# Softmax scaling of a dynamic convolution moved from VectorE to GpSimd, behind the pace of its products

## The chip, the cores and the metric

One core of a Trainium2 chip. The metric is the device time of one execution in microseconds (us), lower is better. All runs told here are fast, with a granted TensorE clock of 0.987 to 1.0. Ratios are the mean time of one kernel's fast runs over that of the other's fast runs of the same rounds, so they are not quite the ratio of the medians that are quoted. Spans in profiles are about 2 us shorter than times.

Names: TensorE is PE in the profile (PEld its weight loads), VectorE is DVE, ScalarE is ACT, GpSimd is POOL, SyncE is SP.

## The reference, cut to what matters

```python
# per token and head: softmax over K = 7 taps, then a weighted sum of 7 shifted rows of x
w = np.exp(weight_gen - max);  w = w / w.sum(-1)            # (8, 4096, 8 heads, 7)
conv = einsum('bshk,bskhg->bshg', w, x_unfolded)            # D = 192 = 8 heads x 24
h = conv.reshape(32768, 192) @ w_in                         # 192 -> 2048
out = (h - tanh(h)) @ w_out                                 # 2048 -> 192
```

## The kernel before

Tokens go through in 32 superblocks of 1024. In iteration n of the main loop, TensorE makes the first matmul of superblock n (16 tiles `ph`), the second matmul of superblock n-1 (into `obank`), and, at the seventh of eight pairs of tiles, the sums of superblock n+1 (`conv`: the products are added up while they are transposed, into `pc`). ScalarE does tanh, exp and copies, VectorE does `h - tanh(h)` (`gt`) and the softmax of superblock n+3, GpSimd the seven products of superblock n+2 and an accumulating transfer that adds the odd products to the even ones. The "pace" is an ordering: GpSimd's work for superblock n+2 may not start before VectorE's second subtraction of iteration n.

```python
def softmax_norm(n, bank, in_psum=False):
    e_t, zsum = softmax_sum(n)                    # reduction on VectorE
    zr = bank[:, 512 - J * H : 512]               # a corner of the PSUM bank of the sums
    nc.vector.reciprocal(zr, zsum[:])
    ...
    wsm = wgpool.tile([P, J, H, K], FP32, name="wsm")
    last_wsm[0] = scale(nc.vector, wsm[:], e_t, zr)
    wsm_of[n] = (wsm, wsm_v)
...
# in products(n, ..., behind): 7 multiplications on GpSimd
            if k == 0 and behind is not None:
                order(mul, behind, "pace")        # not before the second subtraction of the iteration
...
for n in range(NTOT):
    if n + 3 < NTOT:
        load_wg(n + 3)
        load_x(n + 3)                             # xpool has 2 buffers: waits for products(n + 1)
    for p in range(J):
        gemm1(n, 2 * p)
        gemm1(n, 2 * p + 1)
        ...
        if p == 0 and 1 <= n < NTOT - 2:
            products(n + 2, behind=last_sub[0] if n > 1 else None)
        if n + 1 < NTOT:
            if p == (6 if n > 0 else 7):
                conv(n + 1, (0, 1))
            if p == (6 if n > 1 else 7):
                bank = conv(n + 1, (2,))
        ...
        if p == (7 if n == 1 else 6) and n + 3 < NTOT:
            softmax_norm(n + 3, bank if n > 0 else obank[0])
```

The `ph` and `pc` tiles share three PSUM buffers in rotation.

The softmax here doesn't subtract the row's maximum and nothing guards it: scores larger than these inputs give would overflow.

Of the kernel before, what the change touches and what calls it, by code (L numbers as in the profile page):

```python
# [8 lines left out]
FP32 = mybir.dt.float32  # L9
# [7 lines left out]
def kernel(  # L17
# [8 lines left out]
    nc = tc.nc  # L26

    B, S, D = x.shape
    H, K = weight_gen.shape[2], weight_gen.shape[3]
    G = D // H  # L30
    F = moe_w_in.shape[1]
    P = nc.NUM_PARTITIONS
# [3 lines left out]
    J = 8  # L36
# [4 lines left out]
    NTOT = B * NSB  # L41
# [11 lines left out]
    wgpool = ctx.enter_context(tc.tile_pool(name="wgpool", bufs=2))  # L53
# [11 lines left out]
    obank = [psum_o.tile([P, 512], FP32, name=f"obank{i}", tag=f"obank{i}") for i in range(2)]  # L65
# [6 lines left out]
    wsm_of = {}  # L72
# [8 lines left out]
    def order(inst, other, reason):  # L81
        tc.add_manual_dep(
            inst.ins,
            other.ins.name,
            mybir.DependencyInfo(mybir.DependencyClass.Sync, mybir.DependencyReason.DATA),
            reason=reason,
        )
# [44 lines left out]
    def softmax_exp(n):  # L132
        wg_t = wg_of.pop(n)
        e_t = wgpool.tile([P, J, H, K], FP32, name="e_t")
        nc.scalar.activation(  # L135
            out=e_t[:].rearrange("p j h k -> p (j h k)"),
            in_=wg_t[:].rearrange("p j h k -> p (j h k)"),
            func=ACT.Exp,
        )
        e_of[n] = e_t  # L140

    def softmax_sum(n):
        e_t = e_of.pop(n)
        zsum = wgpool.tile([P, J * H], FP32, name="zsum")
        nc.vector.reduce_sum(  # L145
            out=zsum[:], in_=e_t[:].rearrange("p j h k -> p (j h) k"), axis=AX.X
        )
        return e_t, zsum

    def softmax_norm(n, bank, in_psum=False):  # L150

        e_t, zsum = softmax_sum(n)
        zr = bank[:, 512 - J * H : 512]
        nc.vector.reciprocal(zr, zsum[:])  # L154
        wsm_v = None
        if in_psum:
            wsm_v = obank[n % 2][:, 0 : J * H * K].rearrange("p (j h k) -> p j h k", j=J, h=H)
            scale(nc.vector, wsm_v, e_t, zr)
        wsm = wgpool.tile([P, J, H, K], FP32, name="wsm")
        last_wsm[0] = scale(nc.vector, wsm[:], e_t, zr)  # L160
        wsm_of[n] = (wsm, wsm_v)

    def softmax_norm_gpsimd(n):
        e_t, zsum = softmax_sum(n)
        zr = wgpool.tile([P, J * H], FP32, name="zr")
        nc.vector.reciprocal(zr[:], zsum[:])
        wsm = wgpool.tile([P, J, H, K], FP32, name="wsm")
        scale(nc.gpsimd, wsm[:], e_t, zr[:])
        wsm_of[n] = (wsm, None)

    def scale(eng, wsm, e_t, zr):
        return eng.tensor_mul(  # L172
            wsm.rearrange("p j h k -> p (j h) k"),
            e_t[:].rearrange("p j h k -> p (j h) k"),
            zr.rearrange("p (n o) -> p n o", o=1).to_broadcast([P, J * H, K]),
        )

    def products(n, on_vector=(), sums=None, hooks={}, behind=None):
        x_t = x_of.pop(n)
        wsm, wsm_v = wsm_of.pop(n)  # L180
        in_pairs = n not in PLAIN

        even = ppool.tile([P, NPAIR, NC, J, H, GC], BF16, name="even")
        odd = ppool.tile([P, NPAIR, NC, J, H, GC], BF16, name="odd")
        last = ppool.tile([P, NC, J, H, GC], BF16, name="last")
        dst = {}
        for i in range(NPAIR):
            dst[2 * i] = even[:, i]
            dst[2 * i + 1] = odd[:, i]
        dst[K - 1] = last[:]  # L190
        if -1 in hooks:
            hooks[-1]()
        for k in range(K):
            eng, w = (nc.vector, wsm_v) if k in on_vector else (nc.gpsimd, wsm[:])
            mul = eng.tensor_mul(  # L195
                dst[k].rearrange("p c j h g -> p j h c g"),
                x_t[:, k : k + J, :].rearrange("p j (h c g) -> p j h c g", h=H, c=NC),
                w[:, :, :, k : k + 1]
                .rearrange("p j h (k o) -> p j h k o", o=1)
                .to_broadcast([P, J, H, NC, GC]),  # L200
            )
            if k == 0 and behind is not None:


                order(mul, behind, "pace")
            if k == K - 2 and in_pairs:

                nc.gpsimd.dma_start(  # L208
                    out=even[:].rearrange("p i c j h g -> p (i c j h g)")[:, 0:ACC],
                    in_=odd[:].rearrange("p i c j h g -> p (i c j h g)")[:, 0:ACC],  # L210
                    accum_op=mybir.AluOpType.add,
                    max_dma_last_dim=4096,
                )
            if k in hooks:
                hooks[k]()
        if in_pairs:
            groups = [even[:, i] for i in range(NPAIR)] + [last[:]]
            prods_of[n] = [
                groups + ([odd[:, NPAIR - 1]] if c == NC - 1 else []) for c in range(NC)
            ]  # L220
        else:
            prods_of[n] = [[dst[k] for k in (sums or range(K))]] * NC

    def conv(n, *parts):

        prods = prods_of[n]
        if n not in conv_of:
            conv_of[n] = cpool.tile([P, NC, HT], BF16, name="convT")
        convT = conv_of[n]
        pcs = [psum_h.tile([P, 2, HT], FP32, name="pc", tag="ph") for _ in parts]  # L230

        for gi in range(max(len(g) for g in prods)):
            for chunks, pc in zip(parts, pcs):
                some = [c for c in chunks if gi < len(prods[c])]
                last = gi == max(len(prods[c]) for c in chunks) - 1
                for c in some:
                    for j in range(JH):
                        col = ((c - chunks[0]) * JH + j) * R
                        for r in range(2):
                            nc.tensor.matmul(  # L240
                                pc[:, r, col : col + R],
                                lhsT=prods[c][gi][
                                    r * R : (r + 1) * R, c, 2 * j : 2 * j + 2
                                ].rearrange("p j h g -> p (j h g)"),
                                rhs=ident[r * R : (r + 1) * R, r * R : (r + 1) * R],
                                start=(gi == 0 and c == chunks[0] and j == 0),
                                stop=(last and c == some[-1] and j == JH - 1),
                            )
        for chunks, pc in zip(parts, pcs):
            c0, nch = chunks[0], len(chunks)  # L250
            nc.scalar.activation(  # L251
                out=convT[:, c0 : c0 + nch, :].rearrange("p c (j r t) -> p r (c j) t", r=2, t=R),
                in_=pc[:, :, 0 : nch * JH * R].rearrange("p r (cj t) -> p r cj t", t=R),
                func=ACT.Copy,
            )
        if parts[-1][-1] == NC - 1:
            prods_of.pop(n)
        return pcs[-1][:, 0]

    def gemm1(n, f):  # L260
        convT = conv_of[n]
# [120 lines left out]
    load_wg(0)  # L382
    load_x(0)
    softmax_exp(0)
    softmax_norm(0, obank[0], in_psum=True)
    load_wg(1)
    load_x(1)
    load_w_in(0, FA)
# [4 lines left out]
        hooks={2: rest_of_w_in},  # L393
    )
    softmax_exp(1)
    softmax_norm(1, obank[1], in_psum=True)
    load_wg(2)
    copy_w_in(0, FA, nc.scalar)
    copy_w_in(FA, F, nc.sync)
    products(1, on_vector=(0, 1), hooks={4: load_w_out})  # L400
    conv(0, (0, 1), (2,))
    load_x(2)
# [3 lines that stand above are left out]
            load_x(n + 3)  # L406
# [3 lines that stand above are left out]
            if n == 0 and p == 1:  # L410
                softmax_exp(2)
            if p == 5 and n + 3 < NTOT:
                softmax_exp(n + 3)
            if n >= 1:
                gemm2((n - 1) * J + p)
# [3 lines that stand above are left out]
                if p == (6 if n > 0 else 7):  # L419
                    conv(n + 1, (0, 1))  # L420
                if p == (6 if n > 1 else 7):
                    bank = conv(n + 1, (2,))
            if n == 0 and p == 2:
                softmax_norm_gpsimd(2)
                products(2)
            if p == (7 if n == 1 else 6) and n + 3 < NTOT:

                softmax_norm(n + 3, bank if n > 0 else obank[0])
    gemm2(LAST)
    for j in range(J):  # L430
        gemm2_last(j)
# [30 lines left out]
```

## Time and profile before

| | kernel before |
|---|---|
| time, median of 3 | 772.58 us (771.97 to 773.71) |
| span of the profile | 770.0 us |
| TensorE busy | 96%, and 93% of the chain that ended last |
| one superblock with softmax, in the steady part | 22.82 us |
| the one superblock without (end of the run) | 22.63 us |
| GpSimd idle per superblock, waiting at the pace | 1.18 us |

A superblock's time is read from TensorE: from the start of one superblock's sums to the start of the next ones. The lines are in the prediction.

### The profile page before, as it was taken

To read this page: it belongs to the slowest core of one execution; us is meant where nothing else is said; L and a number is where in the kernel's file an instruction comes from. 1 tells how busy PE (TensorE), PEld (TensorE's weight loads), DVE (VectorE), ACT (ScalarE), POOL (GpSimd) and SP (SyncE) were. 2 spreads that over 40 slices of the span, in tenths; PEclk is the share of its full clock that TensorE was granted. 3 is DMA by queue.
4 is the path that set the end of the run, shared out by engine and by line. 5 is a ranking of instruction groups with operands and counts; after the bars stand their busy time and mean duration, and the time that the engine had idled before them with its cause. 6 is when DMAs were issued, how large, how long until landed. Compare 5 with 4: busy or idle time off the path is not lost.

```text
span 770.0 us, 32309 instructions
## 1 busy us (share of the span) xinstructions
PE 740.4 (96%) x14784; PEld 578.0 (75%) x14784; DVE 668.6 (87%) x624; ACT 640.9 (83%) x865; POOL 668.3 (87%) x261
## 2 busy tenths in 40 slices
PE   2789999999999999999999999999999999999997
PEld 2267777777777777777777778777777777778777
DVE  6978989988989889888988998989889988988883
ACT  1877888888888888888888888888888888888882
POOL 6999999999999999999999999999999999999000
PEclk9999999999999999999999999999999999999999
DMA  7913677665557765556775555775555776542312
GB/s 214 196 63 96 172 182 182 164 143 127 148 147 181 182 152 125 134 149 168 181 177 114 129 155 155 181 178 134 132 142 147 177 181 156 132 118 63 81 43 84
DMA packets 25848, 111.38 MB, mean 145 GB/s; under 512 B 4800, under 2 KB 9456, under 8 KB 21624
## 3 DMA queue, kind: packets, MB, share of 16 engines
q1 hardware_dynamic: 14688, 76.95, 30.1%
q0 software_dynamic: 10816, 31.99, 25.8%
q8 instruction: 115, 1.88, 1.0%
q10 hardware_dynamic: 208, 0.39, 0.2%
q14 instruction: 21, 0.17, 0.1%
HBM read 54.49 MB, written 25.17 MB: 103 GB/s over the span
## 4 chain that ended last, share of the span: by engine, by line
PE 93%; DVE 3%; POOL 1%; DMA 1%; ACT 1%; issue 1%; SPq 0%; POOLq 0%; DVEq 0%
PE ph L265 43%; PE obank L297 43%; PE pc L240 6%; DVE gt L277 2%; PE po L331 1%; DMA x_t<-in_x_dram 1%; POOL even L195 1%; ACT convT L251 0%; ACT th L275 0%; POOL odd L195 0%; DVE wsm L172 0%; DVE zsum L145 0%; SPq L117 0%; DVE pc L154 0%; DVE obank L154 0%
## 5 line engine op out<-in xcount | busy, mean ns | idle before, releaser
L277 DVE TENSOR_TENSOR gt<-ph,th 128x1024 bf16<-128x1024 f32 x512 | 602.5, 1219 | 63.9 <-ACT th L275 63.6
L275 ACT ACTIVATE th<-ph 128x1024 f32<-128x1024 f32 x512 | 497.3, 1022 | 64.3 <-PE ph L265 63.6
L265 PE MATMUL ph<-convT,w_in 64*128 64x512 bf16 x3072 | 385.5, 377 | 7.5 <-DVE gt L277 5.3
L297 PEld LDWEIGHTS <-gt 64*128 64x128 bf16 x7936 | 344.2, 94 | 52.8 <-issue 1.1
L297 PE MATMUL obank<-w_out,gt 64*128 64x192 bf16 x7936 | 373.9, 243 | 1.8 <-issue 0.9
L195 POOL TENSOR_TENSOR even<-x_t,wsm 128x1536 bf16<-128x1536 f32 x94 | 276.8, 2945 | 29.3 <-DVE gt L277 28.2
L195 POOL TENSOR_TENSOR odd<-x_t,wsm 128x1536 bf16<-128x1536 f32 x93 | 273.8, 2945 | 0.0
L265 PEld LDWEIGHTS <-w_in 64*128 64x128 bf16 x3072 | 175.8, 94 | 117.2 <-issue 20.4
L195 POOL TENSOR_TENSOR last<-x_t,wsm 128x1536 bf16<-128x1536 f32 x31 | 103.4, 3337 | 0.0
L315 ACT ACTIVATE out_sb<-obank 128x192 f32<-128x192 f32 x248 | 82.2, 331 | 14.1 <-PE obank L297 8.7
L251 ACT ACTIVATE convT<-pc 128x1024 bf16<-128x1024 f32 x64 | 48.6, 808 | 30.8 <-PE pc L240 30.8
L240 PE MATMUL pc<-ident,even 64*128 64x64 bf16 x2304 | 47.3, 191 | 3.0 <-DVE gt L277 1.5
L240 PEld LDWEIGHTS <-even 64*128 64x128 bf16 x2304 | 42.5, 96 | 3.8 <-issue 1.9
L208 POOL DMA_DIRECT2D even<-odd x29 | 34.9, 1205 | 9.0 <-POOL odd L195 9.0
L154 DVE RECIPROCAL pc<-zsum 128x64 f32<-128x64 f32 x28 | 15.7, 561 | 14.8 <-ACT convT L251 14.8
L240 PE MATMUL pc<-ident,odd 64*128 64x64 bf16 x448 | 15.3, 198 | 12.6 <-DVE odd L195 12.4
L135 ACT ACTIVATE e_t<-wg_t 128x448 f32<-128x448 f32 x32 | 18.5, 577 | 7.6 <-DMA wg_t<-in_weight_gen_dram 7.6
L240 PE MATMUL pc<-ident,last 64*128 64x64 bf16 x768 | 23.1, 191 | 0.7 <-issue 0.6
L145 DVE TENSOR_REDUCE zsum<-e_t 128x64 f32<-128x448 f32 x32 | 19.5, 609 | 3.0 <-ACT e_t L135 3.0
L240 PEld LDWEIGHTS <-odd 64*128 64x128 bf16 x448 | 11.3, 100 | 12.9 <-DVE odd L195 12.5
L172 DVE TENSOR_TENSOR wsm<-e_t,pc 128x448 f32<-128x448 f32 x28 | 17.4, 622 | 2.9
L240 PEld LDWEIGHTS <-last 64*128 64x128 bf16 x768 | 16.9, 96 | 1.0 <-issue 0.7
(22 smaller groups left out, 51.4 us busy)
## 6 DMA issues: line engine op xcount, KB each, us to landing
x_t<-in_x_dram SPq DMA_DIRECT2D x24, 1344.0 KB
even<-odd POOLq DMA_DIRECT2D x29, 1024.0 KB, 8.9
out_dram<-out_sb SPq DMA_DIRECT2D x31, 768.0 KB
x_t<-in_x_dram SPq DMA_DIRECT2D x8, 1176.0 KB
wg_t<-in_weight_gen_dram SPq DMA_DIRECT2D x32, 224.0 KB
x_t<-in_x_dram SPq DMA_DIRECT2D x8, 157.5 KB
w_in<-in_moe_w_in_dram POOLq DMA_DIRECT2D x6, 128.0 KB, 6.7
w_out<-in_moe_w_out_dram POOLq DMA_DIRECT2D x1, 768.0 KB, 9.2
```

The source lines that it names most:

```text
L135: nc.scalar.activation(out=e_t[:].rearrange("p j h k -> p (j h k)"), in_=wg_t[:].rearrange("p j h k -> p (j h k)"), func=ACT.Exp,)
L145: nc.vector.reduce_sum(out=zsum[:], in_=e_t[:].rearrange("p j h k -> p (j h) k"), axis=AX.X)
L172: return eng.tensor_mul(wsm.rearrange("p j h k -> p (j h) k"), e_t[:].rearrange("p j h k -> p (j h) k"), zr.rearrange("p (n o) -> p n o", ...
L195: mul = eng.tensor_mul(dst[k].rearrange("p c j h g -> p j h c g"), x_t[:, k : k + J, :].rearrange("p j (h c g) -> p j h c g", h=H, c=NC), ...
L208: nc.gpsimd.dma_start(out=even[:].rearrange("p i c j h g -> p (i c j h g)")[:, 0:ACC], in_=odd[:].rearrange("p i c j h g -> p (i c j h g)" ...
L240: nc.tensor.matmul(pc[:, r, col : col + R], lhsT=prods[c][gi][r * R : (r + 1) * R, c, 2 * j : 2 * j + 2].rearrange("p j h g -> p (j h g)") ...
L251: nc.scalar.activation(out=convT[:, c0 : c0 + nch, :].rearrange("p c (j r t) -> p r (c j) t", r=2, t=R), in_=pc[:, :, 0 : nch * JH * R].re ...
L265: nc.tensor.matmul(ph[:, r, :], lhsT=w_in[r * R : (r + 1) * R, c, f * P : (f + 1) * P], rhs=convT[r * R : (r + 1) * R, c, :], start=(c == ...
L275: last_act[0] = nc.scalar.activation(out=th[:], in_=ph_f, func=ACT.Tanh)
L277: last_sub[0] = nc.vector.tensor_sub(gt[:], ph_f, th[:])
L297: mm = nc.tensor.matmul(po[:, 0:D], lhsT=g_of[n][f][r * R : (r + 1) * R, col : col + P], rhs=w_out[r * R : (r + 1) * R, f, :], start=(r == ...
L315: last_act[0] = nc.scalar.activation(out=out_sb[:, j, :], in_=po[:, 0:D], func=ACT.Copy)
```

## The change

The intent: give VectorE back the scaling (0.62 us per superblock), and put it on GpSimd in the idle time that the pace leaves it. The pace moves from the first product to the scaling ahead of it, and the reciprocal goes to SBUF, where the kernel before already keeps it for superblock 2, the one that GpSimd scales (0.97 us at 35.77 us in the prediction's fourth view).

```diff
-    def softmax_norm(n, bank, in_psum=False):
+    def softmax_norm(n, bank=None):
...
+        wsm = wgpool.tile([P, J, H, K], FP32, name="wsm")
+        if bank is None:
+            zr = wgpool.tile([P, J * H], FP32, name="zr")
+            nc.vector.reciprocal(zr[:], zsum[:])
+            wsm_of[n] = (wsm, None, e_t, zr)
+            return
...
     def products(n, on_vector=(), sums=None, hooks={}, behind=None):
         x_t = x_of.pop(n)
-        wsm, wsm_v = wsm_of.pop(n)
+        wsm, wsm_v, e_t, zr = wsm_of.pop(n)
+        if e_t is not None:
+            first = scale(nc.gpsimd, wsm[:], e_t, zr[:])
+            if behind is not None:
+                order(first, behind, "pace")
...
-            if k == 0 and behind is not None:
-                order(mul, behind, "pace")
...
-            if p == (7 if n == 1 else 6) and n + 3 < NTOT:
-                softmax_norm(n + 3, bank if n > 0 else obank[0])
+            if p == 6 and n + 3 < NTOT:
+                softmax_norm(n + 3)
```

More of the change, by code (lines that the diff above doesn't have):

```diff
@@ L140, in softmax_exp @@
         e_of[n] = e_t
-    def softmax_sum(n):
+    def softmax_norm(n, bank=None):
         e_t = e_of.pop(n)
@@ L147, in softmax_sum @@
         )
-        return e_t, zsum
-    def softmax_norm(n, bank, in_psum=False):
-        e_t, zsum = softmax_sum(n)
+        wsm = wgpool.tile([P, J, H, K], FP32, name="wsm")
[4 more added lines that the diff above has]
+            return
         zr = bank[:, 512 - J * H : 512]
         nc.vector.reciprocal(zr, zsum[:])
-        wsm_v = None
-        if in_psum:
-            wsm_v = obank[n % 2][:, 0 : J * H * K].rearrange("p (j h k) -> p j h k", j=J, h=H)
-            scale(nc.vector, wsm_v, e_t, zr)
-        wsm = wgpool.tile([P, J, H, K], FP32, name="wsm")
-        last_wsm[0] = scale(nc.vector, wsm[:], e_t, zr)
-        wsm_of[n] = (wsm, wsm_v)
-    def softmax_norm_gpsimd(n):
-        e_t, zsum = softmax_sum(n)
-        zr = wgpool.tile([P, J * H], FP32, name="zr")
-        nc.vector.reciprocal(zr[:], zsum[:])
-        wsm = wgpool.tile([P, J, H, K], FP32, name="wsm")
-        scale(nc.gpsimd, wsm[:], e_t, zr[:])
-        wsm_of[n] = (wsm, None)
+        wsm_v = bank[:, 0 : J * H * K].rearrange("p (j h k) -> p j h k", j=J, h=H)
+        scale(nc.vector, wsm_v, e_t, zr)
+        last_wsm[0] = scale(nc.vector, wsm[:], e_t, zr)
+        wsm_of[n] = (wsm, wsm_v, None, None)
     def scale(eng, wsm, e_t, zr):
@@ L194, in products @@
             eng, w = (nc.vector, wsm_v) if k in on_vector else (nc.gpsimd, wsm[:])
-            mul = eng.tensor_mul(
+            eng.tensor_mul(
                 dst[k].rearrange("p c j h g -> p j h c g"),
@@ L257, in conv @@
             prods_of.pop(n)
-        return pcs[-1][:, 0]
     def gemm1(n, f):
@@ L384 @@
     softmax_exp(0)
-    softmax_norm(0, obank[0], in_psum=True)
+    softmax_norm(0, obank[0])
     load_wg(1)
@@ L395 @@
     softmax_exp(1)
-    softmax_norm(1, obank[1], in_psum=True)
+    softmax_norm(1, obank[1])
     load_wg(2)
@@ L421 @@
                 if p == (6 if n > 1 else 7):
-                    bank = conv(n + 1, (2,))
+                    conv(n + 1, (2,))
             if n == 0 and p == 2:
-                softmax_norm_gpsimd(2)
+                softmax_norm(2)
                 products(2)
-            if p == (7 if n == 1 else 6) and n + 3 < NTOT:
-                softmax_norm(n + 3, bank if n > 0 else obank[0])
+            if p == 6 and n + 3 < NTOT:
+                softmax_norm(n + 3)
     gemm2(LAST)
```

## The prediction

> **What bounds the kernel now.** I read the page first: engine shares, then the chain that ended last.
>
> ```profile
> PE 740.4 (96%) x14784; PEld 578.0 (75%) x14784; DVE 668.6 (87%) x624; ACT 640.9 (83%) x865; POOL 668.3 (87%) x261
> PE 93%; DVE 3%; POOL 1%; DMA 1%; ACT 1%; issue 1%; SPq 0%; POOLq 0%; DVEq 0%
> ```
>
> TensorE is busy 96% of the 770.0 us span and carries 93% of the chain. VectorE and GpSimd are at 87%, so a change of theirs pays only where TensorE waits for them. GpSimd stops at 712 us (last product), so inside its stretch it is much fuller than 87%.
>
> The second view is the chain as pieces in time: one superblock with softmax work, from the transposing sums of one superblock (`pc`, x104) to the next, and then the end of the run, where no superblock is left to normalise.
>
> ```profile
> 408.82 1.52 PE pc L240 x104
> ...
> 413.15 0.65 PE ph L265 x6
> 413.80 0.02 issue
> 413.81 0.82 PE ph L265 x6
> ...
> 431.64 1.52 PE pc L240 x104
> ...
> 705.57 1.52 PE pc L240 x104
> ...
> 728.20 1.52 PE pc L240 x104
> ```
>
> Columns: start, length, what. A superblock with softmax takes 431.64 - 408.82 = 22.82 us, the one without 728.20 - 705.57 = 22.63 us. The difference, 0.19 us, sits where a pair of first-matmul tiles breaks into two halves: 0.65 + 0.02 + 0.82 = 1.49 us instead of 1.29 or 1.30 us elsewhere.
>
> The third view, VectorE's timeline around that break, shows why:
>
> ```profile
> 410.22 0.61 DVE L145 TENSOR_REDUCE zsum<-e_t 128x64 f32<-128x448 f32 x1
> 411.34 0.56 DVE L154 RECIPROCAL pc<-zsum 128x64 f32<-128x64 f32 x1 [0.51 <-ACT convT L251]
> 412.00 0.62 DVE L172 TENSOR_TENSOR wsm<-e_t,pc 128x448 f32<-128x448 f32 x1
> 412.54 4.71 DVE L277 TENSOR_TENSOR gt<-ph,th 128x1024 bf16<-128x1024 f32 x4
> ```
>
> The reciprocal is put into the bank of `pc`, so it waits 0.51 us for ScalarE to empty it; the scaling follows, and only then the subtractions. The first one ends near 412.54 + 1.18 = 413.72 (4.71 / 4 = 1.18 each). The three `ph`/`pc` buffers go round, and the second half of the broken pair needs the buffer that this subtraction frees: TensorE goes on at 413.81. ScalarE had the tanh for it ready near 412.2.
>
> The fourth view is GpSimd's timeline.
>
> ```profile
> 35.77 0.97 POOL L172 TENSOR_TENSOR wsm<-e_t,zr 128x448 f32<-128x448 f32 x1
> 36.82 2.90 POOL L195 TENSOR_TENSOR even<-x_t,wsm 128x1536 bf16<-128x1536 f32 x1
> ...
> 394.50 2.90 POOL L195 TENSOR_TENSOR even<-x_t,wsm 128x1536 bf16<-128x1536 f32 x1 [1.18 <-DVE gt L277]
> ...
> 417.33 2.90 POOL L195 TENSOR_TENSOR even<-x_t,wsm 128x1536 bf16<-128x1536 f32 x1 [1.18 <-DVE gt L277]
> ```
>
> In the steady part GpSimd idles 1.18 us of every 22.82, at the pace. It also shows the moved operation once, at superblock 2: 0.97 us long, and 36.82 - 35.77 = 1.05 us until the next starts.
>
> [...] Here it is 0.97 against 0.62 us, 1.56. [...] so I count 1.05 us. [...] The page of the kernel before has such a queue, with 115 packets and 1.88 MB, 16 KB each.
>
> **The change, part by part.**
> 1. 29 scalings leave VectorE (superblocks 3 to 31): 29 x 0.62 = 18.0 us of busy time, of which nearly all lay beside TensorE. On the path it counts as part 3.
> 2. The reciprocal goes to SBUF and no longer waits for `pc`. It can start at about 410.86, behind the reduction, and ends near 411.45, before the tanh is ready (412.2). The subtraction then starts at 412.25 instead of 412.54, ends near 413.44, and TensorE finds its buffer free before 413.62.
> 3. So each softmax superblock should fall to the 22.63 us of the one that has none. Iterations 2 to 28 normalise superblocks 5 to 31: 27 x 0.19 = 5.1 us.
> 4. In iteration 0 there is no second matmul and the chain runs over VectorE (23% of the chain's first 75 us are its subtractions). There the scaling of superblock 3 is on the path, 0.62 us and some 0.06 us of queue: 0.7 us. Superblock 4's softmax moves from the eighth to the seventh pair of iteration 1; VectorE waits for ScalarE about there (2.16 us), so nothing.
> 5. GpSimd gets 29 x 1.05 = 30 us. Behind one another its superblocks take 21.56 us (78.05, 99.62, 121.18 are the starts while it was still late at the beginning, before the pace bound it), so 22.61 us with scaling, against a TensorE superblock of 22.63. The 1.18 us of idle time is used up to within 0.02 us.
>
> Parts 3 and 4 give 5.8 us: 772.6 - 5.8 = 766.8 us if nothing comes in return.
>
> **What comes in return.** GpSimd starts late: it is behind the pace until superblock 7 (a wait of 0.18 us at 143.43) and catches up only through its idle 1.18 us. In the new kernel there is nothing to catch up with. Working it from superblock 3: its products end at 79.1 (78.05 + 1.05), superblock 4's at 79.1 + 22.6 = 101.7, while the mark that superblock 5 waits for comes at about 96: a lag of about 5.5 us that persists.
>
> The sums themselves can stand it: the accumulating transfer is issued 17.5 us after the pace (412.00 - 394.50), lands 8.9 us later, and is needed 37.1 us after the pace; 10.7 - 1.05 - 5.5 leaves about 4 us. But the next x load starts when products end, and it slides against TensorE. In the steady part it starts 15.5 us before the sums (393.35 to 408.82); with the lag, about 9. Then the burst of x load, output store and accumulation (DMA up to 390 GB/s in that stretch) lasts into the sums, where TensorE eats instructions fastest (208 in 1.5 us). The old trace has this once, at superblock 4, when GpSimd was still late:
>
> ```profile
> 112.77 0.26 PE L240 MATMUL pc<-ident,last 64*128 64x64 bf16 x6 [0.60 <-issue]
> ```
>
> The x load had started 11.2 us before; TensorE stood 0.60 us for nothing that the profile names, between two instructions of a kind. A 16 KB instruction packet landed at 111.36, just before it went on. Counting TensorE's instructions, its four such breaks after the first 50 us (66.8, 112.0, 341.6, 501.7 us) are all at the same place in a block of 256, so I read them as instruction fetches come late. [...]
>
> Each such stall makes TensorE later and so the lag smaller. It should end once the x load again leads the sums by about 12 us, at a lag near 2.3 us. So the loss is about 5.5 - 2.3 = 3.2 us in all, mostly in the first third, not so much per superblock. The old kernel's 0.6 us at superblock 4 is one of its kind and goes into the exchange: I estimate 772.6 - 5.8 - 0.6 + 3.2 = 769.4, and put 769.2.
>
> **The rivals.**
> - *GpSimd becomes the bound.* For: 22.61 against 22.63. Against: there are 4 us of slack, so at 0.1 us more per superblock 29 of them cost 2.9 us of lag and TensorE would still not wait. At 0.3 us more per superblock it would cost 29 x 0.3 - 4 = 4.7 us: about 771.
> - *No fetch stalls.* For: superblock 3, with the x load 9.9 us before its sums, had none. Then 766 to 767.
> - *Fetch stalls that go on,* at 0.3 us in each of 27 superblocks: 8 us, so 774 to 775. Against: they shorten the lag that causes them.
> - *TensorE finds another wait for the 0.19 us.* Against: the superblock without softmax. Then nothing is gained: 772 to 775.
>
> **Range and chances.** 766.2 is the sum without loss, less a little; 773.2 is the gain eaten by stalls or by GpSimd. 2% is 15.5 us, beyond any sum here: 0.01 for faster, 0.98 for same, 0.01 for slower.
>
> **What would show it.** Right: the reciprocal without a wait for `convT`; a pair of tiles after the sums at 1.29 us, not 1.49; superblocks of 22.63 us; GpSimd's wait for `gt` gone or a few tenths; `issue` stalls of TensorE near the sums, more of them than before, early. Wrong: superblocks still at 22.8 us in the middle; TensorE waiting for GpSimd or for the accumulating transfer; GpSimd's spacing per superblock above 22.7 us; a time above 773.2, which would mean stalls that go on.

Passages on the hardware that no trace or run of this case shows are cut from that text where it is marked. No term of its sum goes with them: it came to 772.6 - 5.8 - 0.6 + 3.2 = 769.4 us, put at 769.2. What the trace of the kernel before shows:

- "Here it is 0.97 against 0.62 us" compares the scaling on GpSimd with that on VectorE. 1.05 us is a spacing from start to start, since GpSimd's lengths overlap: products are 2.90 us long and start 2.86 us apart (397.37 and 400.23 us).
- Part 2 counts no loss for a reciprocal in SBUF. At superblock 2, where the kernel before has it there, it took 0.55 us beside a product (30.53 us); into PSUM it takes 0.56 us.
- "Such a queue" is q8 of the page, kind "instruction". TensorE's 29600 instructions (14784 matmuls, 14784 weight loads, 32 semaphore instructions) over 115 packets are 257 for each.
- The last sentence cut was the ground for "about 12 us", and so for the 3.2 us: with it gone they stand as my estimate. The trace shows landings: an instruction packet landed 11.2 us after the x load of 100.15 us was issued (at 111.36) and one 11.8 us after that of 393.35 us (at 405.19).

## The result, and the profile after

The changed kernel takes 770.58 us (median of 4, 770.22 to 770.86) against 772.82 us (median of 4) before: a ratio of 0.9971, with a 95% interval of 0.9953 to 0.9988. That is a gain of 2.2 us. The prediction said 769.2 us, 766.2 to 773.2.

The changed kernel's page, engine shares and the chain that ended last:

```profile
PE 736.7 (96%) x14784; PEld 583.1 (76%) x14784; DVE 652.9 (85%) x595; ACT 640.8 (83%) x865; POOL 695.2 (90%) x290
PE 93%; DVE 2%; issue 1%; POOL 1%; DMA 1%; ACT 1%; SPq 0%; POOLq 0%
```

About 16 us left VectorE and 27 us came to GpSimd. The chain is still TensorE's. The two profiled executions are 1.3 us apart and not 2.2: the one before took 772.03 us, 0.8 us less than the median.

VectorE's timeline around the sums of one superblock (start, length, instruction, idle time before it and its releaser), after:

```profile
410.67 0.61 DVE L145 TENSOR_REDUCE zsum<-e_t 128x64 f32<-128x448 f32 x1
411.38 0.55 DVE L151 RECIPROCAL zr<-zsum 128x64 f32<-128x64 f32 x1
412.73 2.35 DVE L269 TENSOR_TENSOR gt<-ph,th 128x1024 bf16<-128x1024 f32 x2 [0.79 <-ACT th L267]
```

The reciprocal follows the reduction without the wait for `convT`, and VectorE now idles 0.79 us until the tanh is there: it no longer holds anything up.

The chain as pieces in time, two successive sums, after:

```profile
409.28 1.52 PE pc L233 x104
...
413.60 1.29 PE ph L257 x12
...
431.91 0.97 PE pc L233 x67
432.88 0.27 issue
433.15 0.71 PE pc L233 x37
```

431.91 - 409.28 = 22.63 us, as predicted, and the pair of tiles after the sums takes 1.29 us where it had taken 1.49. The same lines show the other side: after 67 of the 104 matmuls of the second sums TensorE stops. The starts of the two instructions lie 0.46 us apart, and no semaphore is named: "issue".

GpSimd's timeline, after:

```profile
396.45 1.42 POOL L163 TENSOR_TENSOR wsm<-e_t,zr 128x448 f32<-128x448 f32 x1
397.95 2.90 POOL L192 TENSOR_TENSOR even<-x_t,wsm 128x1536 bf16<-128x1536 f32 x1
...
419.09 1.42 POOL L163 TENSOR_TENSOR wsm<-e_t,zr 128x448 f32<-128x448 f32 x1
```

No wait for `gt` is left; GpSimd goes round in 22.64 us without a pause. TensorE's timeline has the largest of its stops:

```profile
68.20 0.90 PE L289 MATMUL obank<-w_out,gt 64*128 64x192 bf16 x17 [1.33 <-issue]
93.11 0.91 PE L289 MATMUL obank<-w_out,gt 64*128 64x192 bf16 x17 [0.80 <-issue]
114.82 0.26 PE L233 MATMUL pc<-ident,last 64*128 64x64 bf16 x6 [1.65 <-issue]
```

The kernel before has three lines with an "issue" of TensorE after 60 us: 0.94 us at 67.97, the 0.60 us of the prediction, and 0.20 us at 341.99.

The balance over the 28 superblocks from the sums near 88 us to those near 727 us, by the starts of the same instructions:

```
                         28 superblocks   of it steady                        excess (stops)
before                   639.69 us        27 x 22.82 + 22.63 = 638.77 us      0.9 us
after                    638.62 us        28 x 22.63         = 633.64 us      5.0 us
```

The steady part is 5.1 us shorter and the stops are 4.1 us longer, 3.8 of the 5.0 us in the first nine of the 28 superblocks.

### The profile page after: what moved, and what is told of

Same layout as the page of the kernel before. It is cut to its first block, busy times and chain, and to the rows that moved or that the text cites. A ratio compares the mean times of both kernels' runs of the same rounds, so it can differ in the third digit from the quotient of the medians.

```text
span 768.7 us, 32330 instructions
## 1 busy us (share of the span) xinstructions
PE 736.7 (96%) x14784; PEld 583.1 (76%) x14784; DVE 652.9 (85%) x595; ACT 640.8 (83%) x865; POOL 695.2 (90%) x290
## 3 DMA queue, kind: packets, MB, share of 16 engines
q8 instruction: 115, 1.88, 1.0%
## 4 chain that ended last, share of the span: by engine, by line
PE 93%; DVE 2%; issue 1%; POOL 1%; DMA 1%; ACT 1%; SPq 0%; POOLq 0%
PE ph L257 43%; PE obank L289 43%; PE pc L233 6%; DVE gt L269 2%; PE po L323 1%; DMA x_t<-in_x_dram 1%; POOL even L192 1%; ACT th L267 0%; ACT convT L244 0%; POOL odd L192 0%; DVE zr L151 0%; DVE zsum L145 0%; SPq L117 0%; SPq L93 0%; SPq L121 0%
## 5 line engine op out<-in xcount | busy, mean ns | idle before, releaser
L192 POOL TENSOR_TENSOR even<-x_t,wsm 128x1536 bf16<-128x1536 f32 x94 | 272.8, 2903 | 3.9 <-DMA x_t<-in_x_dram 1.6
L192 POOL TENSOR_TENSOR odd<-x_t,wsm 128x1536 bf16<-128x1536 f32 x93 | 269.9, 2903 | 0.0
L257 PEld LDWEIGHTS <-w_in 64*128 64x128 bf16 x3072 | 180.1, 94 | 108.4 <-issue 11.8
L163 POOL TENSOR_TENSOR wsm<-e_t,zr 128x448 f32<-128x448 f32 x30 | 41.7, 1390 | 0.0
L233 PE MATMUL pc<-ident,odd 64*128 64x64 bf16 x448 | 15.5, 198 | 13.1 <-DVE odd L192 12.8
L151 DVE RECIPROCAL zr<-zsum 128x64 f32<-128x64 f32 x30 | 16.6, 553 | 3.0
```

Of the source, the lines that this page charges most:

```text
L163: return eng.tensor_mul(wsm.rearrange("p j h k -> p (j h) k"), e_t[:].rearrange("p j h k -> p (j h) k"), zr.rearrange("p (n o) -> p n o", ...
L192: eng.tensor_mul(dst[k].rearrange("p c j h g -> p j h c g"), x_t[:, k : k + J, :].rearrange("p j (h c g) -> p j h c g", h=H, c=NC), w[:, : ...
L233: nc.tensor.matmul(pc[:, r, col : col + R], lhsT=prods[c][gi][r * R : (r + 1) * R, c, 2 * j : 2 * j + 2].rearrange("p j h g -> p (j h g)") ...
L257: nc.tensor.matmul(ph[:, r, :], lhsT=w_in[r * R : (r + 1) * R, c, f * P : (f + 1) * P], rhs=convT[r * R : (r + 1) * R, c, :], start=(c == ...
```

## The experiments

The theory: (a) the gain is VectorE's wait for the `pc` bank, 0.19 us per superblock; (b) the loss is instruction fetches of TensorE that come late, because GpSimd never catches up with its pace and its lateness pushes the x loads into the sums. The rivals: GpSimd as the bound, the moved pace itself, a wait that the profile does not name, something else in the loads. The experiments came in three calls; each was timed beside the kernel before on the same chip (medians 772.45, 772.78 and 772.43 us). All gave correct results.

### e1: the kernel before, reciprocal to SBUF, scaling stays on VectorE

```diff
-        zr = bank[:, 512 - J * H : 512]
+        if n > 1:
+            zr = wgpool.tile([P, J * H], FP32, name="zr")[:]
+        else:
+            zr = bank[:, 512 - J * H : 512]
```

> The kernel before with one edit: from superblock 5 on the reciprocal goes to SBUF, the scaling stays on VectorE. If the 0.19 us per superblock came only from the reciprocal's wait for the pc bank, superblocks fall from 22.82 to 22.63 us, GpSimd keeps about 1 us idle at the pace, and the time is about 767.8 us (772.8 - 27 x 0.19). If[...] a VectorE operation with two SBUF inputs contends with GpSimd's reads, the scaling of 0.62 us or the product beside it grows by up to 2.9 us, the first subtraction comes late, and superblocks stay at or above 22.8 us: 772.8 us or more.

That the two would contend was an assumption, put to the test here; the 2.9 us is the length of one product (2.90 us).

The edit works from superblock 3 on, not 5; the text is wrong there. Measured: 771.06 us (770.64 to 771.35), ratio 0.9979 (0.9966 to 0.9991), between the two forecasts, since both effects are there. VectorE's timeline, at superblock 4 and in the steady part:

```profile
72.38 3.02 DVE L175 TENSOR_TENSOR wsm<-e_t,zr 128x448 f32<-128x448 f32 x1
...
413.02 0.85 DVE L175 TENSOR_TENSOR wsm<-e_t,zr 128x448 f32<-128x448 f32 x1
```

With both inputs in SBUF the scaling took 3.02 us and, for superblock 5, 2.52 us, beside GpSimd's product, instead of 0.62 us with the reciprocal in PSUM, and TensorE waited 1.91 us for the subtraction behind the first. Later it starts only 0.37 us before the end of a product (413.39 us), behind which GpSimd issues its transfer (413.69 us), and takes 0.85 us, and superblocks take 22.63 us. So the 0.19 us is the wait for the bank: it goes without the scaling leaving VectorE. And the start of the run pays for the long scalings: the sums near 88 us start 3.3 us later than in the kernel before (91.62 instead of 88.33), which is why the time is not 767.8 us.

### e2: the kernel before, with idle work on GpSimd

```diff
+        if n >= 3:
+            idle = wgpool.tile([P, J, H, K], FP32, name="idle")
+            first = nc.gpsimd.tensor_mul(idle, wsm, wsm)     # 448 elements, unused
+            if behind is not None:
+                order(first, behind, "pace")
...
-            if k == 0 and behind is not None:
-                order(mul, behind, "pace")               # the pace moves with it, as in the change
```

> The kernel before plus one idle GpSimd multiplication of 448 elements per superblock from 3 on, behind the pace: the cost on GpSimd without the gain on VectorE. My theory (GpSimd stays late, x loads slide into the sums, instruction fetches come late): superblocks of 22.82 us, more stalls of TensorE near the sums in the first half, 1.5 to 4 us in all, so 774 to 777 us. Rival (GpSimd's extra work is free within its 1.18 us of idle time, the stalls in the changed kernel have another cause): 772.8 us, no new stalls.

Measured: 773.91 us (773.62 to 774.54), ratio 1.0018 (1.0005 to 1.003): 1.5 us slower, just under the range that I gave. Superblocks are at 22.82 us in the steady part, the stops over the 28 superblocks are 3.0 us instead of 0.9, at 92, 113 and 184 us above all: the places where the changed kernel has them. The load on GpSimd alone brings stops, without any change on VectorE.

### e4: the changed kernel, x loads held back until the sums are done

```diff
-            load_x(n + 3)
+            if n < 2:
+                load_x(n + 3)
...
                     conv(n + 1, (2,))
+                    if 2 <= n < NTOT - 3:
+                        load_x(n + 3, last_conv[0])   # its large loads wait for the copy of the sums
```

> The changed kernel, with the x loads from superblock 5 on held until the sums of that iteration are emptied, so that no x load runs into sums, however late GpSimd is. My theory: the stalls of TensorE after superblock 5 (about 3.5 us in the changed kernel's trace) go, 767 to 768 us. Rival (the stalls come from something else, GpSimd's lateness by itself or the accumulating transfer): 770.6 us as the changed kernel. If x now comes too late for the products, GpSimd waits for x_t and falls back, over 771 us.

Measured: 766.11 us (766.01 to 766.56), ratio 0.9917 (0.9903 to 0.9931). GpSimd's times are those of the changed kernel within 0.1 us (scaling at 419.00 instead of 419.09), while TensorE runs ahead: GpSimd's scaling starts 4.9 to 5.4 us behind its pace all through, where in the changed kernel the lag falls from 5.0 to 0.7 us. Yet all superblocks from the sums near 88 us on take 22.63 us, except one of 22.75. The lateness by itself costs nothing; the transfers that it moves do. The gain is larger than forecast, since the stops at 92 and 113 us went too: the load of superblock 5 had lain beside the first.

The edit moves more than x. On SyncE's timeline, in the changed kernel, the output store and the load of the softmax weights are issued right behind the x load that waits for its buffer; in e4 they no longer follow it:

```profile
396.98 0.33 SPq L107 DMA_DIRECT2D x_t<-in_x_dram  x1
397.35 1.39 SPq L311 DMA_DIRECT2D out_dram<-out_sb  x1
398.79 1.02 SPq L93 DMA_DIRECT2D wg_t<-in_weight_gen_dram  x1
```

```profile
408.08 0.33 SPq L108 DMA_DIRECT2D x_t<-in_x_dram  x1
408.50 0.38 SPq L94 DMA_DIRECT2D wg_t<-in_weight_gen_dram  x1
412.87 0.34 SPq L314 DMA_DIRECT2D out_dram<-out_sb  x1
```

(The sums before them start at 386.5 us in the changed kernel and at 405.4 us in e4.) No experiment tells the three apart. For the stop at 433 us of the changed kernel, the packets under way in the trace between the end of the instruction block before (428.39 us) and the start of the late instruction packet (430.81 us) are 720 KB of the store, 189 KB of x and 120 KB of the weights. So where this document says that x loads bring stops, the store and the weights queued behind them are meant too.

### e5: scaling on GpSimd only from superblock 11 on

```diff
-                softmax_norm(n + 3, bank if n > 0 else obank[0])
+                if n + 3 >= FROM:                     # FROM = 11
+                    softmax_later(n + 3)              # the changed kernel's way
+                else:
+                    softmax_norm(n + 3, bank if n > 0 else obank[0])
```

> The kernel before for superblocks up to 10 (scaling on VectorE), the changed one's way from 11 on (scaling on GpSimd behind the pace), when GpSimd has caught up. My theory: superblocks fall to 22.63 us from iteration 8 on (21 x 0.19 = 4.0 us) and no new stalls come since GpSimd is not late: 768.8 us, within 0.8. Rival (GpSimd's scaling brings stalls by itself, late or not): 770 us or more.

Measured: 768.85 us (767.72 to 770.11), ratio 0.9946 (0.9932 to 0.9959). The time is the forecast one, and superblocks from iteration 8 on take 22.63 us. But "no new stops" was wrong: the profiled execution, the slowest of the five, has stops of 1.6 us at 341 us and 0.6 us at 473 us, where GpSimd kept its pace (the scalings before them start 0.07 us after the end of the subtraction that they wait for). Both lie at the end of a block of 256 instructions, as all stops of e9 below do (in the kernel before, counts 12737 and 17857, each 193 more than a multiple of 256, come at 341.6 and 472.9 us). Being late makes stops likelier (5.0 us of them over the changed kernel's 28 superblocks, 0.9 us before); it isn't a condition for them. Why these two, and not the same places in the other executions, stays open.

### e3: the changed kernel without the pace

```diff
-                products(n + 2, behind=last_sub[0] if n > 1 else None)
+                products(n + 2)
```

> The changed kernel without the pace. My theory: GpSimd never reaches the pace in the changed kernel (its trace has no wait for gt left), so taking the pace away changes nothing: 770.6 us, within 0.6. Rival (the moved pace still holds GpSimd back and matters): 1 us or more of difference either way.

Measured: 770.57 us (770.25 to 771.09), ratio 0.9972 (0.9959 to 0.9986), against 0.9971 with the pace. In the changed kernel the pace does nothing.

### e6: the changed kernel, scaling twice

```diff
             first = scale(nc.gpsimd, wsm[:], e_t, zr[:])
+            if n >= 3:
+                again = wgpool.tile([P, J, H, K], FP32, name="again")
+                scale(nc.gpsimd, again[:], e_t, zr[:])       # unused
```

> The changed kernel with a second, unused scaling on GpSimd per superblock from 3 on: the rival in which GpSimd is the bound, made true. GpSimd's superblock should take 22.64 + 1.05 = 23.7 us, its last products end near 57 + 29 x 23.7 = 744 us instead of 714, and TensorE waits for them: 790 us, within 4. If instead there were slack beyond what I count, TensorE would still go at 22.63 and the time stay under 780 us.

Measured: 789.44 us (788.79 to 789.61), ratio 1.0214 (1.02 to 1.0228). The time is the forecast one, the way to it isn't. GpSimd goes round in 23.40 us (the two scalings are only 0.93 us apart). TensorE does not wait for it by name; from the view of waits:

```profile
PE pc L236 <- issue: 17.7, 14, 2.2
```

(total, times, longest.) GpSimd holds TensorE back through the stops: they follow the lateness, about as much as it grows (23.40 - 22.63 = 0.77 us for each of 29 superblocks, 22 us; TensorE's waits for "issue" between 60 and 760 us are 17.7 + 2.7 + 1.5 = 21.9 us), and TensorE's superblocks come to 23.4 us on average.

### e10: e6 with the x loads behind the sums

> The kernel of e6 (a second, unused scaling on GpSimd) with the x loads behind the sums. In e6 TensorE lost 19 us, all of it in stalls at block boundaries and none in waits for GpSimd. My theory: without those stalls TensorE goes at 22.63 us until GpSimd, at 23.4 us per superblock, has used up some us of slack, and then waits for the accumulating transfer or the last products by name: about 784 us. Rival (slack is enough): 766 us.

The edit is e6's and e4's together. Measured: 784.93 us (784.72 to 785.03), ratio 1.0162 (1.0146 to 1.0177). Now TensorE waits for GpSimd's work by name:

```profile
PEld L239 <- POOL even L198: 7.9, 7, 1.7
PE pc L239 <- DMA even<-odd: 6.8, 10, 2.5
```

This is the rival "GpSimd becomes the bound", made true. It needs 0.8 us more per superblock than the change gives GpSimd; in the changed kernel itself no such wait is in the trace after the first 60 us. Some stops into the sums remain, although x now goes behind them:

```profile
PE pc L239 <- issue: 3.2, 7, 0.7
```

For the one that ends at 437.94 us, the packets under way between the end of the block before and the late instruction packet are 524 KB of the accumulating transfer, which GpSimd, later still, has moved towards the sums, and none of x. So it is not x alone that can do this.

### e7: the kernel before, x loads behind the sums

> The kernel before with x loads behind the sums from superblock 5 on, as in e4. My theory: only its own stalls near the sums after the first 90 us go (0.9 us in the trace), superblocks stay 22.82 us: 771.6 us, and the changed kernel with the same edit (766.1) is 5.5 us faster, which is the 5.8 us that the prediction gave for the change without stalls. Rival (holding the x loads back helps by something else than the stalls): it gains the kernel before as much as the changed one, 4 us, so 768.3 us.

The edit is that of e4, on the kernel before. Measured: 771.44 us (771.11 to 771.68), ratio 0.9983 (0.997 to 0.9995). All its superblocks now take 22.82 us and the last 22.63. Holding x back gives the kernel before 1.3 us and the changed one 4.2 us (ratios 0.9971 to 0.9917). With x held back in both, the change is worth 0.9983 - 0.9917 = 0.0066 of 772.6 us, 5.1 us: the prediction's gain of 5.8 us without stops, nearly.

### e8: e4 with the load of superblock 4 held back too

```diff
-            if n < 2:
+            if n < 1:
...
-                    if 2 <= n < NTOT - 3:
+                    if 1 <= n < NTOT - 3:
```

> e4 with the x load of superblock 4 held back too. My theory: the stall of 1.4 us at 66.8 us, inside the second matmul of iteration 1 while the x load of superblock 4 runs, goes: about 764.9 us. Rival: x of superblock 4 then lands too late for its products at 79 us and GpSimd waits a little, without effect on TensorE since that has some us of slack; or the stall stays[...]: 766.1 us.

Measured: 764.93 us (764.67 to 765.09), ratio 0.9899 (0.9883 to 0.9914). The best version, 7.9 us below the kernel before in the same rounds. The chain of TensorE is now without a stop; its sums:

```profile
87.48 1.52 PE pc L236 x104
110.11 1.52 PE pc L236 x104
132.74 1.52 PE pc L236 x104
```

All 28 superblocks take 22.63 us.

### e9: the changed kernel, TensorE's program shifted by 64 instructions

```diff
+    warm = psum_h.tile([P, 2, HT], FP32, name="warm", tag="ph")
+    for i in range(32):
+        nc.tensor.matmul(warm[:, 0, 0:P], lhsT=ident[:], rhs=ident[:],
+                         start=(i == 0), stop=(i == 31))
```

> The changed kernel with 32 idle matmuls (64 TensorE instructions with their weight loads) put before everything, while TensorE has nothing to do yet. If the stalls without a named cause are instruction fetches, they stay at count 193 of a block of 256 TensorE instructions and so move by 64 instructions against the program; time 770.6, within 2 us, since other blocks now fall into the sums. Rival (they belong to a place in the program, a wait that the profile does not show): they stay at the program's places, so at count 193 + 64 = 257, that is 1 of the next block.

Measured: 770.37 us (769.93 to 770.76), ratio 0.9975 (0.9959 to 0.9992). In the changed kernel, counting TensorE's instructions from the start (matmuls, weight loads and its 32 semaphore instructions; without these the count drifts), the eight stops after 60 us with no named cause (0.28 us or more from start to start) lie at counts 1729, 2753, 3521, 5313, 6337, 8129, 16321 and 19137; each is 193 more than a multiple of 256. With 64 instructions put ahead, the seven that are left are again all at 193 (1729, 2753, 4545, 6337, 9153, 12737, 15553), none at 257. The first has moved from the second matmul into the sums and has grown:

```profile
68.43 0.24 PE L233 MATMUL pc<-ident,last 64*128 64x64 bf16 x5 [3.39 <-issue]
```

The stops belong to blocks of 256 instructions, not to places in the program. A packet of 16 KB on the instruction queue lands 1.3 to 1.6 us before TensorE goes on each time (at 113.32 us for the stop that ends at 114.82 us). That queue is q8 of the changed kernel's page, kind "instruction" (115 packets, 1.88 MB), so I read the stops as instruction fetches that come late.

## Why the prediction was right

- **The gain per superblock** (part 3, 27 x 0.19 = 5.1 us): right. Steady superblocks went from 22.82 to 22.63 us, the wait of the reciprocal is gone, and e1 shows that this wait was the cause.
- **Iteration 0** (part 4, 0.7 us): right in kind, a little large. Between the same two TensorE instructions, in its first sums and at the end of iteration 0's, the time went from 31.67 to 31.13 us, 0.5 us. In the profile it doesn't show at 88 us, where the changed kernel is 0.15 us behind: its first x landed 0.4 us later in that execution, and the stop near 67 us is 0.4 us longer.
- **GpSimd's superblock** (part 5): 22.61 us forecast, 22.64 measured. From start to start the scaling takes 1.50 us here and not 1.05, but 0.42 us of it comes back at the transfer (from the sixth product's start to the transfer's start 3.20 us, where the late superblocks of the kernel before had 3.62): the round grows by 1.07 us.
- **GpSimd not the bound**: right, and shown by e6 and e10 with their named waits or stops only at 23.4 us.
- **The lateness that persists**: right, smaller than forecast. Superblock 5's scaling starts at 102.11 us, 4.0 us behind the end of the subtraction that is its pace (forecast 5.5); superblock 19's at 419.09, 1.4 us behind, and the last one's 0.7 us (forecast 2.3 at the end). In e4, without the stops, the lag stays near 5 us, as the prediction worked out for that case.
- **Stops that shorten the lateness and so die out**: mostly right. The x load leads the sums by 8.7 us at first (79.98 to 88.65) and by 12.3 us at 409 us, the 12 us forecast, and the stops become rare. They don't end: 0.46 us at 433 us and 1.1 us at 502 us came later.
- **The mis-sized term** is the loss. The prediction put 3.2 - 0.6 = 2.6 us net; over the 28 superblocks it was 5.0 - 0.9 = 4.1 us. The loss was taken as the fall of the lag, from 5.5 to 2.3 us; the lag fell from 5.0 us (superblock 4) to 0.7, since stops still came at leads of some 12 us. That, with the little that iteration 0 gave, is why the time is 770.6 and not 769.2 us.
- **The rivals**: "no stops" (766 to 767 us) is what the changed kernel would be without them: e4 has 766.1. "Stops that go on at 0.3 us" did not come in the changed kernel; in e6, where the lateness is renewed with each superblock, it did.

## What to carry to other kernels

Before filling an engine's idle time, ask what that idle time does: here it let GpSimd catch up, and with it held the x loads, and what is queued behind them, away from the sums, where TensorE goes through its instructions fastest (208 in 1.52 us, where the second matmul has 64 in 1.32 us). A load that is released by "buffer free" moved here with the engine that frees it (it led the sums by 8.7 us at first in the changed kernel, by 15.5 us in the steady part before), and took along what stood behind it in its queue; tied instead to the engine on the critical path, after its densest stretch, the same loads were worth 4.2 us (e4) and 5.6 us (e8) to the changed kernel. A stop between two equal instructions with no semaphore behind it is worth counting out against the instruction blocks, of 256 here.
